# Result rows moved to partitions 30-33 and 94-97 and stored by two queues, wo's first set in two pieces, five loads in halves of 64 partitions

## The chip, the cores and the metric

The kernel runs on one core of one Trainium2 chip. The metric is the device time of one execution in microseconds. Before the change it is 218.12 us, the median of three runs (217.67 to 219.65).

## What is computed

Two sequences (B = 2) each decode one token. Attention over a window of a cached history is multiplied by a gate that comes from a small gated MLP, and the input is added:

```python
xn = _layernorm(x, axis=-1)
s = _A_ref(xn, A_k_cache, A_v_cache, A_wq, A_wo)
g = _silu(_B_ref(xn, B_w_in, B_w_sp, B_b_sp, B_w_out))
return x + s * g
```

The attention `_A_ref` has 32 query heads and 8 key and value heads of 128 elements, and looks at the last W = 4096 positions of the cache:

```python
q = (x @ wq).reshape(B, Sq, Hq, Dh)          # D = 512 -> 32 x 128
...
scores = einsum("bhqd,bhkd->bhqk", q, k) * (Dh ** -0.5)
p = _softmax(scores, axis=-1)
o = einsum("bhqk,bhkd->bhqd", p, v)
return o.reshape(B, Sq, Hq * Dh) @ wo        # 4096 -> 512
```

The gate's branch `_B_ref` takes xn through w_in (512 x 1792) and a GELU, normalizes one half of the result, scales it by w_sp and b_sp, multiplies it by the other half, and takes it through w_out (896 x 512). Everything is float32. The weights wq and wo have 8.4 MB each, and the windows of k and v 33.6 MB each. They are read once; there is next to no reuse, since only two rows are multiplied with every weight.

## The kernel before

The whole program is one pass without a loop on the chip; the Python loops are unrolled, and `InOrder` (lines 27 to 39) keeps each engine's instructions in the order in which the source writes them. Its helper's line 37 therefore stands for nearly every instruction in the profile.

**Loads.** Large loads are issued on SP's queue (`sp`). Its order is win, wout, two tiles of wq, then the tiles of k and v for the eight key heads ("units"), then wo in two sets. Tiles of win, wq, k, v and wo take turns in a ring of four buffers (`slot`, line 83; RING = 4), so that a load waits until the readers of the tile four places before it are done; wout has a place of its own. Each tile covers all 128 partitions, with one contiguous run of DRAM for each partition. Small loads (xs, which is x as two rows; wb1; x4, which is x as eight rows of 128) are issued on ACT's queue.

**Units.** For each unit, DVE transposes the k tile in four parts (`turn`, the tile kt), PE multiplies them with the prepared queries (`scores`), DVE, PE and ACT make the softmax (`probabilities`), and PE multiplies the probabilities with the v tile (`values`, into acc). `evacuate` scales acc into o, `collect` gathers o over the partitions into col, and `spread` moves the heads' outputs into oT, the weights of the product with wo. SETS (line 329) says which units share an oT: units 0 to 3, 4 and 5, 6 and 7.

**Weights of 32 columns.** The products with wo, wout and the group sums use four groups of 32 output partitions each (G = 4). Only B = 2 of 32 columns of such a weight are not zero. In hT and oT these are columns 0 and 16 of each 32, so that the results stand on partitions 32g and 32g + 16. `rowm` (line 155) has a one where the partition's number modulo 32 is the column's number; multiplied with it, the four groups of a tile are added up.

**The end.** wo's rows arrive as a first set (16 blocks for units 0 to 3, one load of 4096 KB) and a second one (16 blocks for the other units, in loads of 4, 4, 4, 2, 1 and 1 blocks), lines 476 to 485. `wo_early` multiplies whole blocks of 512 columns into part, four blocks side by side; the first 24 of the 32 blocks go that way, after the last unit's `gathered` and `spread_after`. ACT copies part to parts, PE adds its groups up into so with rowm, and the last eight blocks are added to so one quarter of the columns after another (lines 516 to 523). DVE multiplies so by the gate (which is ready long before) and adds x4, and one store on SP writes the eight rows, on partitions 0, 16, 32 and so on, to the output.

Of the kernel before, what the change touches and what calls it, by code (L numbers as in the profile page):

```python
# [9 lines left out]
F32 = mybir.dt.float32  # L10
# [4 lines left out]
P = 128  # L15
HQ, DH = 32, 128
G = 4
# [25 lines left out]
def kernel(  # L43
# [13 lines left out]
    nc = tc.nc  # L57
    pe, dve, act, sp = (InOrder(tc, e) for e in (nc.tensor, nc.vector, nc.scalar, nc.sync))
    B, _, D = x.shape
    _, HKV, SK, _ = k_cache.shape  # L60
# [7 lines left out]
    FT = FH // P  # L68
    NJ = HQ * DH // P
    DC = D // G  # L70
# [7 lines left out]
    cst = ctx.enter_context(tc.tile_pool(name="cst", bufs=1))  # L78
    ring = ctx.enter_context(tc.tile_pool(name="ring", bufs=RING))
    sb = ctx.enter_context(tc.tile_pool(name="sb", bufs=2))  # L80
    ps = ctx.enter_context(tc.tile_pool(name="ps", bufs=1, space=bass.MemoryType.PSUM))

    def slot(name, *shape):
        return ring.tile([P, *shape], F32, tag="slot", name=name)

    def bank(name, *shape):
        return ps.tile([P, *shape], F32, tag="kt", name=name, bufs=3)
# [5 lines left out]
    win = slot("win", KT, F)  # L93
    sp.dma_start(win, win_v)
    wout = cst.tile([P, FT, D], F32, tag="wout", name="wout")
    sp.dma_start(wout, w_out.rearrange("(p j) d -> p j d", p=P))
    wq_v = wq.rearrange("(p k) f -> p k f", p=P)
    wqt = []
    for a in range(0, KT, 2):
        t = slot(f"wq{a}", 2, HQ * DH)  # L100
        sp.dma_start(t, wq_v[:, a : a + 2, :])
        wqt += [t[:, 0], t[:, 1]]

    wb1 = cst.tile([1, 2], F32, tag="wb1", name="wb1")
    act.dma_start(wb1[:, 0:1], bass.AP(tensor=w_sp.tensor, offset=w_sp.offset, ap=[[1, 1], [1, 1]]))
    act.dma_start(wb1[:, 1:2], bass.AP(tensor=b_sp.tensor, offset=b_sp.offset, ap=[[1, 1], [1, 1]]))
    x4 = cst.tile([P, DC], F32, tag="x4", name="x4")
    nc.gpsimd.memset(x4, 0.0)
    by_group = [[DC, G], [D, B], [1, DC]]
    act.dma_start(x4[0 : P : P // (G * B), :], bass.AP(tensor=x.tensor, offset=x.offset, ap=by_group))  # L110

    def load(name, src, u):
        t = slot(f"{name}{u}", NT, DH)
# [16 lines left out]
    for n in range(HKV):  # L130
        p = Unit()
# [17 lines left out]
    nc.gpsimd.memset(xnT, 0.0)  # L149
    ones = cst.tile([P, P], F32, tag="ones", name="ones")  # L150
    nc.gpsimd.memset(ones, 1.0)
    hT = cst.tile([P, FT, 32], F32, tag="hT", name="hT")
    nc.gpsimd.memset(hT, 0.0)

    rowm = cst.tile([P, 32], F32, tag="rowm", name="rowm")
    dve.tensor_reduce(rowm, ident.rearrange("p (g c) -> p c g", g=G), axis=AX.X, op=ALU.add)

    def rsqrt(dst, a, tag):
# [19 lines left out]
    pt = bank("xnT_ps", KT, B)  # L178
# [39 lines left out]
    for k in range(KT):  # L218
        for n in range(G):
# [3 lines left out]
                start=(k == 0), stop=(k == KT - 1),  # L223
# [14 lines left out]
    def queries(k):  # L238
        for r in range(NR):
            for g in range(G):  # L240
                c = (r * G + g) * 512
                pe.matmul(
                    pq[r][32 * g : 32 * g + 32, :], xnT[:, k, :], wqt[k][:, c : c + 512],
                    start=(k == 0), stop=(k == KT - 1),
                )
# [14 lines left out]
    z1, z2, w2 = zT[:, 0], zT[:, 1], u[:, 0]  # L260
# [16 lines left out]
    rsqrt(mean, var, "z")  # L277
    dve.tensor_mul(z2, z2, free_ap(mean, 0, per_b))
    dve.tensor_scalar(z2, z2, wb[:, 0:1], wb[:, 1:2], op0=ALU.mult, op1=ALU.add)
    dve.tensor_mul(hT[:, :, 0 : 16 * B : 16], z1, z2)  # L280
    queries(2)
    place4 = place(4, 2)
    place2 = place(2, 4)
    py = bank("ys", D)
    for j in range(FT):
        g = j % G
        pe.matmul(py[32 * g : 32 * g + 32, :], hT[:, j, :], wout[:, j, :], start=(j < G), stop=(j + G >= FT))
    ys = sb.tile([P, D], F32, tag="o", name="ys", bufs=1)
    act.activation(ys, py, AF.Copy)
    y = bank("y", DC)  # L290
    for g in range(G):
        pe.matmul(y[32 * g : 32 * g + 32, :], rowm, ys[:, g * DC : (g + 1) * DC], start=True, stop=True)
    gate = cst.tile([P, DC], F32, tag="gate", name="gate")
    dve.tensor_scalar(gate, y, -1.0, 80.0, op0=ALU.mult, op1=ALU.min)
    act.activation(gate, gate, AF.Exp)
# [7 lines left out]
    for r in range(NR):  # L303
        src = pq[r].rearrange("p (i d) -> p i d", i=REP)
# [5 lines left out]
    for r in range(NR):  # L310
        pt = bank(f"qT_ps{r}", REP, G, 32)
# [4 lines left out]
    for j in range(G):  # L316
        pe.matmul(
            pw[:, j, :], selj[:, j].rearrange("p g c -> p (g c)"), qT.rearrange("p r g b i -> p (r g b i)"),
            start=True, stop=True,
# [10 lines left out]
    sets = {}  # L330
    for i, (kv, n, nj) in enumerate(SETS):
        o1 = cst.tile([P, B, 32], F32, tag=f"o1_{i}", name=f"o1_{i}")
        oT = cst.tile([P, nj, 32], F32, tag=f"oT_{i}", name=f"oT_{i}")
        nc.gpsimd.memset(oT, 0.0)
        for a in range(n):
            sets[kv + a] = (a, n, o1)
        sets[f"oT{i}"] = (o1, oT, nj)
# [49 lines left out]
    def values(p):  # L387
        p.acc = ps.tile([P, CH, DH], F32, tag="acc", name=f"acc{p.n}")
        n = CT // CH
        for i in range(n):  # L390
            for c in range(CH):
                t = CT * c + CH * i
                pe.matmul(
                    p.acc[32 * c : 32 * c + 32].rearrange("p a d -> p (a d)"),
                    free_ap(p.pT, 32 * CH * i + c, [[CH, 32]]),
                    p.v[:, t : t + CH, :].rearrange("p t d -> p (t d)"), start=(i == 0), stop=(i == n - 1),
                )

    def evacuate(p, split=False):
        p.o = sb.tile([P, CH, DH], F32, tag="o", name=f"o{p.n}", bufs=1)  # L400
        for a in range(CH):
            if split and a % 2:
                dve.tensor_scalar_mul(p.o[:, a, :], p.acc[:, a, :], p.w[:, a : a + 1])
            else:
                act.activation(p.o[:, a, :], p.acc[:, a, :], AF.Copy, scale=p.w[:, a : a + 1])
# [3 lines left out]
    def collect(p):  # L409
        a0, n, o1 = sets[p.n]  # L410
        if a0 == 0:
            col[0] = ps.tile([P, CH, 32], F32, tag="col", name=f"col{p.n}")
        for g in range(G):
            pe.matmul(
                col[0][32 * g : 32 * g + 32], selw[:, SL - E * a0 : SL - E * a0 + 32], p.o[:, :, 32 * g : 32 * g + 32],
                start=(a0 == 0), stop=(a0 == n - 1),
            )
        if a0 == n - 1:
            both = sb.tile([P, 32], F32, tag="both", name=f"both{p.n}", bufs=1)
            dve.reduce_sum(both, col[0].rearrange("p a j -> p j a"), axis=AX.X)  # L420
            dve.tensor_mul(o1, free_ap(both, 0, [[0, B], [1, 32]]), free_ap(ofb, 0, [[1, B], [0, 32]]))

    def spread(i):
        o1, oT, nj = sets[f"oT{i}"]
        t = {8: place2, 16: place4}[nj]
        nx = 32 // nj
        pt = bank(f"oT_ps{i}", B, nj)
        for x in range(nx):
            pe.matmul(
                pt, t[:, x].rearrange("p n h g x -> p (n h g x)"), o1[:, :, nj * x : nj * x + nj],  # L430
                start=(x == 0), stop=(x == nx - 1),
            )
        dve.tensor_copy(oT[:, :, 0 : 16 * B : 16], pt.rearrange("p b j -> p j b"))

    ends = {kv + n - 1: i for i, (kv, n, nj) in enumerate(SETS)}
    def gathered(p):
        if p is not None:
            collect(p)
# [33 lines left out]
    wo_s = []  # L472
# [3 lines left out]
    blocks = []  # L476
    for first, of in ((0, (0,)), (1, (1, 2))):
        t = slot(f"wo{first}", 16, D)
        a = 0
        for i in of:  # L480
            nj = SETS[i][2]
            for j, n in (((0, 16),), ((0, 4), (4, 4)), ((0, 4), (4, 2), (6, 1), (7, 1)))[i]:
                sp.dma_start(t[:, a : a + n, :], wo_s[i][:, j : j + n, :])
                blocks.append((t[:, a : a + n, :], sets[f"oT{i}"][1], j))
                a += n
    EARLY = 24
    done = 0

    def wo_early(n):
        nonlocal done  # L490
        t, oT, j = blocks[n]
        for a in range(t.shape[1]):
            g = done % G
            pe.matmul(
                part[32 * g : 32 * g + 32, :], oT[:, j + a, :], t[:, a, :], start=(done < G), stop=(done >= EARLY - G)
            )
            done += 1

    part = ps.tile([P, 512], F32, tag="s", name="part", bufs=2)
# [4 lines left out]
    gathered(units[-2])  # L504
    values(units[-1])
    evacuate(units[-1], split=True)
    gathered(units[-1])
    spread_after(units[-1])
    for n in range(3):
        wo_early(n)  # L510
    parts = sb.tile([P, D], F32, tag="o", name="parts", bufs=1)
    act.activation(parts, part, AF.Copy)
    so = bank("so", DC)
    for g in range(G):
        pe.matmul(so[32 * g : 32 * g + 32, :], rowm, parts[:, g * DC : (g + 1) * DC], start=True, stop=False)
    for n in range(3, len(blocks)):
        t, oT, j = blocks[n]
        for a in range(t.shape[1]):
            for g in range(G):
                pe.matmul(  # L520
                    so[32 * g : 32 * g + 32, :], oT[:, j + a, :], t[:, a, g * DC : (g + 1) * DC],
                    start=False, stop=(j + a == oT.shape[1] - 1),
                )
    res = cst.tile([P, DC], F32, tag="res", name="res")
    dve.tensor_mul(res, so, gate)
    dve.tensor_add(res, res, x4)
    sp.dma_start(bass.AP(tensor=out.tensor, offset=out.offset, ap=by_group), res[0 : P : P // (G * B), :])


# [26 lines left out]
```

## Time and profile before

| | |
|---|---|
| median of three runs | 218.12 us (217.67 to 219.65) |
| the profiled execution | 218.11 us |
| its span, first to last instruction | 216.2 us |
| mean granted TensorE clock | 0.783 |
| read from HBM | 89.40 MB |
| share of 16 DMA engines that SP's queue (q1) takes | 96.8% |
| DVE busy, PE busy | 103.9 us, 136.8 us |

The page gives, for each engine, its busy time and the share of the span. The span is then cut into 40 slices, with one digit for the busy share of each. The chain that ended last is followed back from the last instruction, each step to what released it. In the list of DMA issues the last number is the time from the issue to the landing, which includes the time that the load stood in the queue behind others. In a timeline, what stands in square brackets is the idle time of the engine before that row and what ended it.

### The profile page before, as it was taken

Reading aid. Unit: us, or ns where it says so; the run is one execution under the profiler, and the core shown is the slowest. Engines: PE = TensorE matmul, PEld = TensorE weight load, DVE = VectorE, ACT = ScalarE, POOL = GpSimd, SP = SyncE. Lnnn points to the kernel's source line nnn. Section 1 sums busy time; section 2 is a strip of 40 time slices with the busy share of each in tenths; the row PEclk is TensorE's granted clock in tenths of the full one; section 3 lists DMA queues with packets and bytes.
Section 4 is the critical chain, followed back from the end, with each engine's and each line's share of the span. In section 5 each row is a group of like instructions: output and inputs, shape, how many; then the busy total and the mean of one; then the engine's idle time right before and its main releaser. Section 6 shows DMA issues by size and latency. Waiting matters only on the chain.

```text
span 216.2 us, 2192 instructions
## 1 busy us (share of the span) xinstructions
PE 136.8 (63%) x908; PEld 46.8 (22%) x908; DVE 103.9 (48%) x161; ACT 23.9 (11%) x60; POOL 3.2 (1%) x16
## 2 busy tenths in 40 slices
PE   0172294627765964984593298359667749969683
PEld 0120021113112222222131122122221122342331
DVE  2504014439539638728908921990487197220201
ACT  5003003200001011021021002101010012030010
POOL 5000000000000000000000000000000000000000
PEclk9998569985587595596599559956955787997998
DMA  7999999999999999999999999999999999999990
GB/s 255 425 437 467 406 455 418 423 443 412 455 400 461 409 455 412 436 430 424 449 403 455 412 449 415 430 436 418 455 408 449 418 443 415 443 430 402 409 376 27
DMA packets 3929, 89.54 MB, mean 414 GB/s; under 512 B 446, under 2 KB 462, under 8 KB 848
## 3 DMA queue, kind: packets, MB, share of 16 engines
q1 hardware_dynamic: 3900, 89.40, 96.8%
q8 instruction: 7, 0.11, 0.2%
q10 hardware_dynamic: 20, 0.01, 0.0%
q14 instruction: 2, 0.02, 0.0%
HBM read 89.40 MB, written 0.00 MB: 413 GB/s over the span
## 4 chain that ended last, share of the span: by engine, by line
DMA 62%; DVE 17%; PE 17%; SPq 2%; issue 1%; ACT 0%; DVEq 0%; ACTq 0%
DMA v<-in_A_v_cache_dram 29%; DMA k<-in_A_k_cache_dram 20%; DVE kt L37 13%; DMA wo<-in_A_wo_dram 12%; PE acc L37 9%; PE s L37 7%; SPq L37 2%; PE pp L37 1%; DVE sm L37 1%; DVE pT L37 1%; DVE qw L37 1%; ACT p L37 0%; DVE mg L37 0%; DVE res L37 0%; PE so L37 0%
## 5 line engine op out<-in xcount | busy, mean ns | idle before, releaser
L37 DVE STREAM_TRANSPOSE kt<-k 128x2048 f32<-128x2048 f32 x32 | 72.7, 2293 | 3.4 <-DMA k<-in_A_k_cache_dram 3.4
L37 PE MATMUL acc<-v,pT 128*32 128x512 f32 x256 | 45.3, 863 | 10.9 <-DMA v<-in_A_v_cache_dram 9.6
L37 PE MATMUL s<-kt,qw 128*32 128x512 f32 x256 | 41.1, 684 | 3.7 <-DVE kt L37 3.1
L37 PE MATMUL pp<-p,swap 128*128 128x512 f32 x16 | 12.6, 880 | 21.0 <-ACT p L37 21.0
L37 DVE CUSTOM_DVE_ANT_1 sm<-s,own 128x512 f32<-128x512 f32 x8 | 5.5, 690 | 36.9 <-PE s L37 36.9
L37 PEld LDWEIGHTS acc<-v,pT 128*32 128x32 f32 x256 | 11.5, 159 | 37.4 <-issue 33.4
L37 ACT ACTIVATE o<-acc,wd 128x128 f32<-128x128 f32 x30 | 8.7, 368 | 73.9 <-PE acc L37 67.1
L37 PE MATMUL q_ps<-wq,xnT 128*32 128x512 f32 x64 | 9.6, 723 | 11.2 <-DMA wq<-in_A_wq_dram 11.2
L37 PEld LDWEIGHTS s<-kt,qw 128*32 128x32 f32 x256 | 9.4, 122 | 33.0 <-issue 21.9
L37 ACT ACTIVATE p<-sm,nb 128x512 f32<-128x512 f32 x8 | 5.8, 723 | 69.1 <-DVE nb L37 69.1
L37 DVE STREAM_TRANSPOSE pT<-pp 128x512 f32<-128x512 f32 x8 | 5.7, 706 | 5.8 <-PE pp L37 5.8
L37 PE MATMUL z<-win,xnT 128*32 128x448 f32 x32 | 5.6, 868 | 4.4 <-DMA win<-in_B_w_in_dram 4.4
L37 PE MATMUL mo<-mg,same 128*128 128x16 f32 x16 | 3.2, 273 | 7.7 <-DVE mg L37 7.7
L37 PEld LDWEIGHTS pp<-p,swap 128*128 128x128 f32 x16 | 3.0, 234 | 21.8 <-ACT p L37 21.8
L37 DVE TENSOR_REDUCE both<-col 128x32 f32<-128x128 f32 x3 | 0.9, 292 | 13.4 <-PE col L37 13.4
L37 PEld LDWEIGHTS mo<-l,same 128*128 128x128 f32 x16 | 4.4, 276 | 6.0 <-issue 6.0
L37 ACT ACT_TABLE_LOAD x4 | 5.1, 1283 | 2.6 <-POOL place L206 2.6
L37 PE MATMUL part<-wo,oT 128*32 128x512 f32 x48 | 5.4, 594 | 0.0
L37 PEld LDWEIGHTS q_ps<-wq,xnT 128*32 128x32 f32 x64 | 1.9, 125 | 14.7 <-DMA wq<-in_A_wq_dram 11.4
L37 PE MATMUL xnT_ps<-ident,xn 2*128 2x2 f32 x4 | 0.6, 253 | 7.0 <-DVE xn L37 7.0
L37 PE MATMUL qj_ps<-qT,selj 128*128 128x64 f32 x8 | 2.0, 428 | 4.8 <-DVE qT L37 4.8
L37 DVE STREAM_TRANSPOSE zt<-z 128x448 f32<-128x448 f32 x1 | 1.0, 975 | 8.3 <-ACT z L37 8.3
(106 smaller groups left out, 66.9 us busy)
## 6 DMA issues: line engine op xcount, KB each, us to landing
k<-in_A_k_cache_dram SPq DMA_DIRECT2D x8, 4096.0 KB, 26.4
v<-in_A_v_cache_dram SPq DMA_DIRECT2D x8, 4096.0 KB, 29.7
wq<-in_A_wq_dram SPq DMA_DIRECT2D x2, 4096.0 KB, 24.2
wo<-in_A_wo_dram SPq DMA_DIRECT2D x1, 4096.0 KB
win<-in_B_w_in_dram SPq DMA_DIRECT2D x1, 3584.0 KB, 11.1
wo<-in_A_wo_dram SPq DMA_DIRECT2D x3, 1024.0 KB, 21.7
wout<-in_B_w_out_dram SPq DMA_DIRECT2D x1, 1792.0 KB, 14.9
wo<-in_A_wo_dram SPq DMA_DIRECT2D x1, 512.0 KB
```

The lines of the kernel that those rows point to most:

```text
L37: return self.tc.keep_in_program_order(call(*args, **kwargs))
```

## The change

- The helper `halves` issues a load as two, for partitions 0 to 63 and 64 to 127. It is used for wout, both tiles of wq, and the two pieces of wo's first set, which was one load of 16 blocks and is now two of eight.
- hT, oT and rowm get 30 columns of zeros ahead of them (PAD). `turn_of` takes a window of 32 columns from them, which starts either at the padding or behind it, so that the two result rows stand on the last two partitions of an even group or on the first two of an odd one. The rows of the result are then on partitions 30 to 33 and 94 to 97.
- x4 is loaded by two issues of four rows each on ACT, and the result is stored by two of four rows, one on ACT and one on SP.
- The blocks list has one more entry, since wo's first set is two pieces. The first piece's `wo_early` moves ahead of the last unit's `gathered`; the others stay behind its `spread_after`.

```diff
--- before.py
+++ after.py
@@ -80,6 +80,10 @@
     sb = ctx.enter_context(tc.tile_pool(name="sb", bufs=2))
     ps = ctx.enter_context(tc.tile_pool(name="ps", bufs=1, space=bass.MemoryType.PSUM))
 
+    def halves(dst, src):
+        for r in (slice(0, P // 2), slice(P // 2, P)):
+            sp.dma_start(dst[r], src[r])
+
     def slot(name, *shape):
         return ring.tile([P, *shape], F32, tag="slot", name=name)
 
@@ -93,21 +97,29 @@
     win = slot("win", KT, F)
     sp.dma_start(win, win_v)
     wout = cst.tile([P, FT, D], F32, tag="wout", name="wout")
-    sp.dma_start(wout, w_out.rearrange("(p j) d -> p j d", p=P))
+    halves(wout, w_out.rearrange("(p j) d -> p j d", p=P))
     wq_v = wq.rearrange("(p k) f -> p k f", p=P)
     wqt = []
     for a in range(0, KT, 2):
         t = slot(f"wq{a}", 2, HQ * DH)
-        sp.dma_start(t, wq_v[:, a : a + 2, :])
+        halves(t, wq_v[:, a : a + 2, :])
         wqt += [t[:, 0], t[:, 1]]
 
     wb1 = cst.tile([1, 2], F32, tag="wb1", name="wb1")
     act.dma_start(wb1[:, 0:1], bass.AP(tensor=w_sp.tensor, offset=w_sp.offset, ap=[[1, 1], [1, 1]]))
     act.dma_start(wb1[:, 1:2], bass.AP(tensor=b_sp.tensor, offset=b_sp.offset, ap=[[1, 1], [1, 1]]))
+    PAD = 32 - B
+    PAIRS = ((act, 0), (sp, 2))
+    pair = lambda t, g: t[32 * g + PAD : 32 * g + PAD + 2 * B, :]
+    of_pair = lambda t, g: bass.AP(tensor=t.tensor, offset=t.offset + g * DC, ap=[[DC, 2], [D, B], [1, DC]])
     x4 = cst.tile([P, DC], F32, tag="x4", name="x4")
     nc.gpsimd.memset(x4, 0.0)
-    by_group = [[DC, G], [D, B], [1, DC]]
-    act.dma_start(x4[0 : P : P // (G * B), :], bass.AP(tensor=x.tensor, offset=x.offset, ap=by_group))
+    for _, g in PAIRS:
+        act.dma_start(pair(x4, g), of_pair(x, g))
+
+    def turn_of(t, j, g):
+        return t[:, 32 * j + PAD * (g % 2) : 32 * j + PAD * (g % 2) + 32]
+
 
     def load(name, src, u):
         t = slot(f"{name}{u}", NT, DH)
@@ -149,10 +161,12 @@
     nc.gpsimd.memset(xnT, 0.0)
     ones = cst.tile([P, P], F32, tag="ones", name="ones")
     nc.gpsimd.memset(ones, 1.0)
-    hT = cst.tile([P, FT, 32], F32, tag="hT", name="hT")
+    hT = cst.tile([P, PAD + 32 * FT], F32, tag="hT", name="hT")
     nc.gpsimd.memset(hT, 0.0)
 
-    rowm = cst.tile([P, 32], F32, tag="rowm", name="rowm")
+    rowp = cst.tile([P, PAD + 32], F32, tag="rowp", name="rowp")
+    nc.gpsimd.memset(rowp, 0.0)
+    rowm = rowp[:, PAD:]
     dve.tensor_reduce(rowm, ident.rearrange("p (g c) -> p c g", g=G), axis=AX.X, op=ALU.add)
 
     def rsqrt(dst, a, tag):
@@ -277,19 +291,19 @@
     rsqrt(mean, var, "z")
     dve.tensor_mul(z2, z2, free_ap(mean, 0, per_b))
     dve.tensor_scalar(z2, z2, wb[:, 0:1], wb[:, 1:2], op0=ALU.mult, op1=ALU.add)
-    dve.tensor_mul(hT[:, :, 0 : 16 * B : 16], z1, z2)
+    dve.tensor_mul(hT[:, PAD:].rearrange("p (j c) -> p j c", c=32)[:, :, :B], z1, z2)
     queries(2)
     place4 = place(4, 2)
     place2 = place(2, 4)
     py = bank("ys", D)
     for j in range(FT):
         g = j % G
-        pe.matmul(py[32 * g : 32 * g + 32, :], hT[:, j, :], wout[:, j, :], start=(j < G), stop=(j + G >= FT))
+        pe.matmul(py[32 * g : 32 * g + 32, :], turn_of(hT, j, 1), wout[:, j, :], start=(j < G), stop=(j + G >= FT))
     ys = sb.tile([P, D], F32, tag="o", name="ys", bufs=1)
     act.activation(ys, py, AF.Copy)
     y = bank("y", DC)
     for g in range(G):
-        pe.matmul(y[32 * g : 32 * g + 32, :], rowm, ys[:, g * DC : (g + 1) * DC], start=True, stop=True)
+        pe.matmul(y[32 * g : 32 * g + 32, :], turn_of(rowp, 0, g), ys[:, g * DC : (g + 1) * DC], start=True, stop=True)
     gate = cst.tile([P, DC], F32, tag="gate", name="gate")
     dve.tensor_scalar(gate, y, -1.0, 80.0, op0=ALU.mult, op1=ALU.min)
     act.activation(gate, gate, AF.Exp)
@@ -330,7 +344,7 @@
     sets = {}
     for i, (kv, n, nj) in enumerate(SETS):
         o1 = cst.tile([P, B, 32], F32, tag=f"o1_{i}", name=f"o1_{i}")
-        oT = cst.tile([P, nj, 32], F32, tag=f"oT_{i}", name=f"oT_{i}")
+        oT = cst.tile([P, PAD + 32 * nj], F32, tag=f"oT_{i}", name=f"oT_{i}")
         nc.gpsimd.memset(oT, 0.0)
         for a in range(n):
             sets[kv + a] = (a, n, o1)
@@ -430,7 +444,7 @@
                 pt, t[:, x].rearrange("p n h g x -> p (n h g x)"), o1[:, :, nj * x : nj * x + nj],
                 start=(x == 0), stop=(x == nx - 1),
             )
-        dve.tensor_copy(oT[:, :, 0 : 16 * B : 16], pt.rearrange("p b j -> p j b"))
+        dve.tensor_copy(oT[:, PAD:].rearrange("p (j c) -> p j c", c=32)[:, :, :B], pt.rearrange("p b j -> p j b"))
 
     ends = {kv + n - 1: i for i, (kv, n, nj) in enumerate(SETS)}
     def gathered(p):
@@ -479,8 +493,8 @@
         a = 0
         for i in of:
             nj = SETS[i][2]
-            for j, n in (((0, 16),), ((0, 4), (4, 4)), ((0, 4), (4, 2), (6, 1), (7, 1)))[i]:
-                sp.dma_start(t[:, a : a + n, :], wo_s[i][:, j : j + n, :])
+            for j, n in (((0, 8), (8, 8)), ((0, 4), (4, 4)), ((0, 4), (4, 2), (6, 1), (7, 1)))[i]:
+                (sp.dma_start if i else halves)(t[:, a : a + n, :], wo_s[i][:, j : j + n, :])
                 blocks.append((t[:, a : a + n, :], sets[f"oT{i}"][1], j))
                 a += n
     EARLY = 24
@@ -492,7 +506,7 @@
         for a in range(t.shape[1]):
             g = done % G
             pe.matmul(
-                part[32 * g : 32 * g + 32, :], oT[:, j + a, :], t[:, a, :], start=(done < G), stop=(done >= EARLY - G)
+                part[32 * g : 32 * g + 32, :], turn_of(oT, j + a, 1), t[:, a, :], start=(done < G), stop=(done >= EARLY - G)
             )
             done += 1
 
@@ -504,27 +518,29 @@
     gathered(units[-2])
     values(units[-1])
     evacuate(units[-1], split=True)
+    wo_early(0)
     gathered(units[-1])
     spread_after(units[-1])
-    for n in range(3):
+    for n in range(1, 4):
         wo_early(n)
     parts = sb.tile([P, D], F32, tag="o", name="parts", bufs=1)
     act.activation(parts, part, AF.Copy)
     so = bank("so", DC)
     for g in range(G):
-        pe.matmul(so[32 * g : 32 * g + 32, :], rowm, parts[:, g * DC : (g + 1) * DC], start=True, stop=False)
-    for n in range(3, len(blocks)):
+        pe.matmul(so[32 * g : 32 * g + 32, :], turn_of(rowp, 0, g), parts[:, g * DC : (g + 1) * DC], start=True, stop=False)
+    for n in range(4, len(blocks)):
         t, oT, j = blocks[n]
         for a in range(t.shape[1]):
             for g in range(G):
                 pe.matmul(
-                    so[32 * g : 32 * g + 32, :], oT[:, j + a, :], t[:, a, g * DC : (g + 1) * DC],
-                    start=False, stop=(j + a == oT.shape[1] - 1),
+                    so[32 * g : 32 * g + 32, :], turn_of(oT, j + a, g), t[:, a, g * DC : (g + 1) * DC],
+                    start=False, stop=(n == len(blocks) - 1 and a == t.shape[1] - 1),
                 )
     res = cst.tile([P, DC], F32, tag="res", name="res")
     dve.tensor_mul(res, so, gate)
     dve.tensor_add(res, res, x4)
-    sp.dma_start(bass.AP(tensor=out.tensor, offset=out.offset, ap=by_group), res[0 : P : P // (G * B), :])
+    for engine, g in PAIRS:
+        engine.dma_start(of_pair(out, g), pair(res, g))
 
 
 # ---- launch: one core; inputs and outputs as the reference has them ----
```

## The prediction

> **What bounds the kernel now.** I read the page first: busy shares, slices, bytes.
>
> ```profile
> span 216.2 us, 2192 instructions
> ...
> PE 136.8 (63%) x908; PEld 46.8 (22%) x908; DVE 103.9 (48%) x161; ACT 23.9 (11%) x60; POOL 3.2 (1%) x16
> ...
> DMA  7999999999999999999999999999999999999990
> ...
> HBM read 89.40 MB, written 0.00 MB: 413 GB/s over the span
> ...
> DMA 62%; DVE 17%; PE 17%; SPq 2%; issue 1%; ACT 0%; DVEq 0%; ACTq 0%
> ```
>
> No compute engine is near its limit. The DMA engines stand at nine tenths or more in 38 of 40 slices, and 62% of the chain that ended last is transfer. Where the chain passes through DVE or PE it only names what released a buffer; the engines of the DMA had other loads to move meanwhile. The table of stages makes that firm (columns: length, busy time and count of PE, PEld, DVE, ACT, POOL, granted clock, DMA share, GB/s):
>
> ```profile
> 11.00:14.00 3.00, 2.04 (x12) 0.68 (x16) 0.00 (x0) 0.00 (x0) 0.00 (x0) 1.00 0.99 425
> ...
> 24.00:34.00 10.00, 6.53 (x36) 1.83 (x36) 1.03 (x6) 1.14 (x2) 0.00 (x0) 0.68 0.99 429
> ...
> 50.00:80.00 30.00, 22.48 (x116) 6.16 (x115) 18.72 (x22) 1.95 (x6) 0.00 (x0) 0.70 1.01 433
> 80.00:110.00 30.00, 20.19 (x112) 7.01 (x116) 20.70 (x19) 2.77 (x8) 0.00 (x0) 0.66 1.00 428
> 110.00:140.00 30.00, 17.37 (x130) 6.28 (x123) 16.38 (x19) 3.91 (x12) 0.00 (x0) 0.82 1.00 431
> ...
> 200.00:212.00 12.00, 9.07 (x126) 4.10 (x128) 1.40 (x5) 1.07 (x3) 0.00 (x0) 1.00 0.90 365
> ```
>
> From 11 us on the rate is 425 to 433 GB/s with a share of about 1, whatever is being loaded. Time that a load adds or saves is therefore time of the kernel: 89.4 MB at 431 GB/s are 207.4 of the 216.2 us. The rest is the start, some idle DMA near 200 to 212 us (a tenth of 12 us, 1.2 us), and the tail. The chain in order of time shows the tail:
>
> ```profile
> 46.65 2.31 DVE kt L37
> ...
> 185.47 26.99 DMA wo<-in_A_wo_dram
> 212.46 0.04 issue
> 212.50 0.47 PE so L37 x8
> ...
> 213.00 0.30 DVE res L37
> ...
> 213.32 0.29 DVE res L37
> ```
>
> The first row is the first transpose of a k tile, which starts when that tile has landed. The last piece of wo lands at 212.46; eight matmuls and two DVE operations follow, then the store.
>
> **The five loads in halves.** Sizes, from the page's list of DMA issues (KB of 1024 bytes, then us to landing):
>
> ```profile
> wq<-in_A_wq_dram SPq DMA_DIRECT2D x2, 4096.0 KB, 24.2
> wo<-in_A_wo_dram SPq DMA_DIRECT2D x1, 4096.0 KB
> win<-in_B_w_in_dram SPq DMA_DIRECT2D x1, 3584.0 KB, 11.1
> wo<-in_A_wo_dram SPq DMA_DIRECT2D x3, 1024.0 KB, 21.7
> wout<-in_B_w_out_dram SPq DMA_DIRECT2D x1, 1792.0 KB, 14.9
> ```
>
> At 431 GB/s a load of 4096 KB (4.194 MB) takes 9.73 us and wout (1.835 MB) 4.26 us. The halved ones are wout, two of wq and wo's first set, which is now two pieces in two halves each: 4.26 + 3 x 9.73 = 33.4 us of the stream, 23.7 of it before k, 9.7 near the end.
>
> No row shows a load that reaches 64 partitions: all the large ones reach 128. So its price must be bounded. The ceiling of 431 GB/s is held either by the sixteen engines that move the bytes or by the partitions that take them, 431/128 = 3.4 GB/s for each. If the engines hold it, halves cost nothing. If the receiving side holds it, a half-load runs at half the rate; the two halves stand behind each other in one queue, whose engines must finish their share of the first before the second, and each load takes twice its time: +33.4 us. A gain at this place has no mechanism, since the share is already 0.99 in these stages and the bytes stay. I take the upper end: 3.4 GB/s is the most that any row here shows a partition to take over a long stretch, and the lower end asks for 6.7, for which there is no row. I keep both ends for the range.
>
> [...]
>
> Rows of wo's first set become 16 KB instead of 32 KB in one run. The nearest rows: wout's 14 KB rows went by in the stage 11 to 14 us and after without a dip (425), and wo's short rows in 200 to 212 gave 365/0.90 = 406 while busy, 6% less. So 0 to 0.6 us; I take 0.1, nearer to wout, whose rows are almost as long.
>
> **More issues and waits on SP.** Six more loads at some 0.5 us of SP each are 3 us in a queue that idles far longer:
>
> ```profile
> SPq L37 <- DVE kt L37: 104.1, 8, 16.1
> ...
> SPq L551 <- DMA out_dram<-res: 0.7, 1, 0.7
> ```
>
> The eight completion semaphores go round faster, so in the built program wq's second half waits for win (0.73 + 11.1 = 11.8 us), with the rest of wq and k behind it on SP; by then wout and wq's first half, 4.26 + 4.87 = 9.1 us of transfer, are still queued. Wo's last two single rows wait for the first piece's two halves, which land at least 8 us before the engines come to those rows. Both cost nothing; without that cover they would cost the whole gap.
>
> **The rows at 30-33 and 94-97.** Every matmul keeps its shape, only the columns of its 32-wide weights move. POOL gets one memset (rowp) ahead of DVE's first reduction, and ACT one more issue ahead of the first activation:
>
> ```profile
> 1.33 0.24 ACTq L37 DMA_DIRECT2D wb<-in_B_w_sp_dram  x1
> ...
> 1.60 0.27 ACTq L37 DMA_DIRECT2D wb<-in_B_b_sp_dram  x1
> ...
> 1.73 0.28 POOL L153 MEMSET hT<- 128x224 f32 x1
> 1.91 0.62 ACTq L37 DMA_DIRECT2D x<-in_A_x_dram  x1
> ...
> 11.96 5.55 PE L37 MATMUL z<-win,xnT 128*32 128x448 f32 x32 [4.35 <-DMA win<-in_B_w_in_dram]
> ```
>
> Behind them wait the layer norm's chain and xnT on DVE, ACT and PE. PE stood idle 4.35 us for win after that chain, which hides 0.28 + 0.62; without this cover they would add up to 0.9.
>
> The store: one issue of 0.69 us on SP for eight lines of 512 bytes becomes one of four lines on SP and one on ACT, side by side.
>
> ```profile
> 213.64 0.69 SPq L37 DMA_DIRECT2D out_dram<-res  x1
> ```
>
> Issues of one line took 0.24 and 0.27, of eight 0.62 and 0.69: four should take about 0.45, so -0.2 us. Bounds: -0.45 (as one line) and +0.5 (the closing wait for a landing, 0.7 in the row above, met twice in part).
>
> **wo's first piece ahead of the last gathering.** PE now does eight blocks of wo's first set before it gathers the last unit, and waits for the first piece there; behind it on PE stand col, the spread of the last set, and the remaining blocks; DVE's both and oT wait for these.
>
> ```profile
> 194.38 5.24 PE L37 MATMUL acc<-v,pT 128*32 128x512 f32 x32
> ...
> 200.92 0.35 DVE L37 TENSOR_SCALAR o<-acc,wd 128x128 f32<-128x128 f32 x1 [0.43 <-ACT o L37]
> ...
> 201.33 0.43 PE L37 MATMUL col<-o,selw 128*32 128x128 f32 x8 [1.71 <-DVE o L37]
> ...
> 203.42 5.36 PE L37 MATMUL part<-wo,oT 128*32 128x512 f32 x48
> ```
>
> Its 16 instructions take 16 x 5.36/48 = 1.8 us and fill the gap in which PE waited for o (199.62 to 201.33). At full rate the piece is there in time: the first 1024 KB piece of wo's second set lands at 183.1 + 21.7 = 204.9 or so (it is issued one SP step after 182.7), the whole first set 2.4 us earlier, its first half 4.9 us before that, at 197.6. At half rate everything up to v's last load is 23.7 us later, acc ends at 223.3, the piece lands at 197.6 + 23.7 + 4.9 = 226.2, and PE waits 2.9 us; col to the start of part is 2.1 us, so all but the second piece is done near 230, that piece lands at 235.9, and the last row of wo at 212.46 + 33.4 = 245.9. The transfer hides this wait by many us, so it costs nothing, and the 1.8 us brought forward gain nothing either: the end still hangs on wo's last row and eight matmuls.
>
> **The sum.** 216.2 + 33.4 + 0.1 - 0.2 = 249.5 us of span. The profiled execution took 218.11 us, 1.9 more than its span and the same as the median 218.12, so **251.4 us**.
>
> **Rivals.** First, on the other side: the engines hold the ceiling, not the partitions, or the halves are dealt to different engines and move together. Then nothing is added: 216.2 + 0.1 - 0.2 + 1.9 = 218.0, with -0.45 to +1.1 for the store and the shorter rows: 217.5 to 219.2. For it: the share and rate are the same for every length of row and every source, as a limit of the engines would be. Against it: the same rows fit a limit of the receiving side just as well, and no row has a partition above 3.4 GB/s. It decides from the first halved load, wout.
>
> Second: two engines that write to the same partitions are served one after the other, not in turn. One then runs ahead by a half-load, the pair works on opposite halves from there on, and the loss is paid once: 4.9 us in wq, up to 2.4 more in wo's shorter halves; 218.0 + 4.9 to 218.0 + 7.3, at most 225.3. For it: the loads of one queue need no common step, as the steady share shows. Against it: nothing shows who would be preferred.
>
> Third: a gain beyond the store. The idle 1.2 us in 200 to 212 and the 0.45 of the store together give 1.65, 216.5; there is no more to win, so over 1% faster (2.2 us) hardly can be.
>
> **Numbers.** A measurement of this kernel tells about 1% from no change: its three runs reach from 217.67 to 219.65. Forecast 0.56, the engines' limit 0.33, loss paid once 0.08, a gain 0.03. I put the forecast ahead because it extends the rate that the rows show for a partition, and not far ahead, because the same rows permit the other. The forecast's own range is 246.0 to 252.5 (engines that are already out of step lose somewhat less; 0.6 for the rows and 0.5 for the store above). Its chance alone doesn't hold 8 in 10, so the range must reach over to the first rival: 217.2 to 252.5. Slower by over 1%: 0.56 + 0.08 = 0.64; within 1%: 0.33; faster: 0.03.
>
> **What would show it.** Right: slices 3 to 8 of the page near 215 GB/s with the DMA share still at nine tenths, wq landing some 24 us later, k's first transpose near 70 us instead of 46.65, and a second dip after v's last load. Wrong: 425 GB/s through these slices, z and q at the same times as before, and an end near 216 us; a store issue not below 0.6 us would make its step wrong alone.

## The result, and the profile after

The changed kernel takes 255.14 us (median of six runs, 253.53 to 256.11) against 218.2 us before: a ratio of 1.168, 95% interval 1.162 to 1.173. The forecast had the direction and the place; the time lies 2.6 us above its range. Ratios and intervals here and below leave out executions over 1.5% above the fastest of their kernel. The profiled execution took 255.21 us, its span is 253.4 us.

The page of the changed kernel, with busy shares, slices, bytes and the chain's shares:

```profile
span 253.4 us, 2208 instructions
...
PE 138.8 (55%) x908; PEld 48.0 (19%) x908; DVE 103.9 (41%) x161; ACT 23.9 (9%) x60; POOL 3.3 (1%) x17
...
DMA  7999999898999999999999999999999999999991
GB/s 290 363 225 240 212 202 222 191 228 275 460 432 419 419 434 442 434 424 419 440 445 422 424 429 437 445 424 419 429 441 440 416 419 429 202 215 219 256 404 45
...
HBM read 89.40 MB, written 0.00 MB: 353 GB/s over the span
...
DMA 65%; PE 16%; DVE 14%; issue 1%; ACT 1%; SPq 1%; another core or an unknown queue 0%; DVEq 0%
```

The bytes are the same, DVE's busy time is the same to a tenth, and the DMA engines look as busy as before. What fell is what they move: some 190 to 240 GB/s in slices 3 to 9, where wout and wq are loaded, and 202 to 256 in slices 35 to 38, where wo's first set is. A row of nines for the DMA engines does not say that they move all they can; it has to be read beside the row of GB/s.

The stages (length, busy time and count of PE, PEld, DVE, ACT, POOL, granted clock, DMA share, GB/s) say the same more sharply:

```profile
24.00:34.00 10.00, 0.00 (x0) 0.00 (x0) 0.00 (x0) 0.00 (x0) 0.00 (x0) 0.50 1.02 213
34.00:44.00 10.00, 2.93 (x16) 0.68 (x16) 0.00 (x0) 0.00 (x0) 0.00 (x0) 0.52 1.00 210
...
104.00:134.00 30.00, 17.31 (x104) 6.30 (x107) 20.37 (x19) 2.77 (x8) 0.00 (x0) 0.69 0.99 428
...
224.00:234.00 10.00, 5.95 (x40) 1.52 (x32) 0.89 (x3) 0.73 (x2) 0.00 (x0) 0.67 0.99 211
```

From 24 to 34 us not one instruction ran on a compute engine, with the DMA share at 1.02 and half the rate of the kernel before (429 in the same stage). Between the two places, in 104 to 134 us, the whole loads run at 428 as ever. The chain in order of time shows where k's first tile is used, and the end:

```profile
14.60 46.61 DMA wq<-in_A_wq_dram
...
70.69 2.31 DVE kt L37
...
229.56 19.78 DMA wo<-in_A_wo_dram
249.34 0.04 issue
249.38 0.47 PE so L37 x8
...
250.20 0.29 DVE res L37
```

k's first transpose starts at 70.69 instead of 46.65, 24.0 later; wo's last row lands at 249.34 instead of 212.46, 36.9 later. The chain passes from wo to wo at 229.56 because SP waited there for a completion semaphore that one of the first pieces still held, and issued wo's last row only then. That wait is no cost: with the share at 0.99 the engines had other rows to move. The tail has its own row in the timeline:

```profile
250.52 0.78 SPq L37 DMA_DIRECT2D out_dram<-res  x1
250.52 0.66 ACTq L37 DMA_DIRECT2D out_dram<-res  x1
```

From the store's issue to the end of the span are 253.4 - 250.5 = 2.9 us, against 216.2 - 213.6 = 2.6 before.

### The profile page after: what moved, and what is told of

Same layout as the page of the kernel before. It is cut to its first block, busy times and chain, and to the rows that moved or that the text cites. A ratio compares the mean times of both kernels' runs of the same rounds, so it can differ in the third digit from the quotient of the medians.

```text
span 253.4 us, 2208 instructions
## 1 busy us (share of the span) xinstructions
PE 138.8 (55%) x908; PEld 48.0 (19%) x908; DVE 103.9 (41%) x161; ACT 23.9 (9%) x60; POOL 3.3 (1%) x17
## 4 chain that ended last, share of the span: by engine, by line
DMA 65%; PE 16%; DVE 14%; issue 1%; ACT 1%; SPq 1%; another core or an unknown queue 0%; DVEq 0%
DMA v<-in_A_v_cache_dram 25%; DMA wq<-in_A_wq_dram 18%; DMA wo<-in_A_wo_dram 17%; DVE kt L37 10%; PE acc L37 7%; PE s L37 5%; DMA win<-in_B_w_in_dram 5%; PE pp L37 1%; PE q_ps L37 1%; DVE pT L37 1%; DVE sm L37 1%; DVE gate L37 1%; PE ys L37 1%; ACT p L37 1%; SPq L37 1%
## 5 line engine op out<-in xcount | busy, mean ns | idle before, releaser
L37 PE MATMUL acc<-v,pT 128*32 128x512 f32 x256 | 44.6, 860 | 15.0 <-DMA v<-in_A_v_cache_dram 14.4
L37 PE MATMUL s<-kt,qw 128*32 128x512 f32 x256 | 38.8, 653 | 4.5 <-DVE kt L37 3.1
L37 PE MATMUL q_ps<-wq,xnT 128*32 128x512 f32 x64 | 10.4, 780 | 37.2 <-DMA wq<-in_A_wq_dram 37.2
L37 PEld LDWEIGHTS acc<-v,pT 128*32 128x32 f32 x256 | 11.4, 158 | 41.8 <-issue 36.6
L37 PE MATMUL part<-wo,oT 128*32 128x512 f32 x48 | 9.9, 987 | 7.4 <-DMA wo<-in_A_wo_dram 7.4
L37 PE MATMUL z<-win,xnT 128*32 128x448 f32 x32 | 4.6, 731 | 5.2 <-DMA win<-in_B_w_in_dram 5.2
L37 DVE TENSOR_TENSOR res<-so,gate 128x128 f32<-128x128 f32 x1 | 0.3, 290 | 13.3 <-PE so L37 13.3
```

The lines of the kernel that those rows point to most:

```text
L37: return self.tc.keep_in_program_order(call(*args, **kwargs))
```

## The experiments

Each kernel was timed beside the kernel before on the same chip. Edits are against the changed kernel where nothing else is said.

### All but the halves

```diff
     def halves(dst, src):
-        for r in (slice(0, P // 2), slice(P // 2, P)):
-            sp.dma_start(dst[r], src[r])
+        sp.dma_start(dst, src)
```

> All of the change but the halves: wout, both tiles of wq and the two pieces of wo's first set are each one load again. Receiving side (a load to partitions 0-63 or 64-127 runs at half rate, and this is the whole cost): 218.2 + 0.3 for the tail, which is 0.3 us longer in the profile of the changed kernel, so 218.5, between 217.8 and 219.3, and 425 to 435 GB/s in every slice. Rival (the 3.7 us beyond the forecast come from the rest: the wait for wo's first piece ahead of the last gathering, the faster round of the semaphores, the moved rows): 221 to 222.

Measured: 218.47 us against 218.15, ratio 1.001 (0.9994 to 1.0026). The stage of wq is back at its rate:

```profile
24.00:34.00 10.00, 6.82 (x36) 1.91 (x36) 1.03 (x6) 0.96 (x2) 0.00 (x0) 0.66 0.99 429
```

So the halves are the whole loss, and the 3.7 us beyond the forecast are theirs too. The moved rows, the two stores, the two pieces and the earlier matmuls together cannot be told from nothing.

### The early halves alone, and the late ones alone

```diff
-                (sp.dma_start if i else halves)(t[:, a : a + n, :], wo_s[i][:, j : j + n, :])
+                sp.dma_start(t[:, a : a + n, :], wo_s[i][:, j : j + n, :])
```

> Halves only in wout and wq; wo's two pieces are whole. Receiving side: k's later tiles stood 25.1 us later in the changed kernel than before, so 218.5 + 25.1 = 243.6 (242.5 to 244.5), and the DMA share stays near 1 while the rate is about 210 GB/s. By the forecast's sizes alone: 218.5 + 23.7 = 242.2.

Measured: 243.48 us, ratio 1.115 (1.111 to 1.119); 25.0 us more than without any halves.

```diff
-    halves(wout, w_out.rearrange("(p j) d -> p j d", p=P))
+    sp.dma_start(wout, w_out.rearrange("(p j) d -> p j d", p=P))
...
-        halves(t, wq_v[:, a : a + 2, :])
+        sp.dma_start(t, wq_v[:, a : a + 2, :])
```

> Halves only in the two pieces of wo's first set. By the forecast's size: 218.5 + 9.7 = 228.2. If the late part of the changed kernel is as large by itself (36.9 - 25.0 = 11.9 us between v's sixth load and the last of wo): 230.4, with v's last load landing about 2 us later than the load before it lets expect.

Measured: 229.86 us (227.33 to 230.66), ratio 1.051 (1.044 to 1.057); 11.4 us more than without halves. The two add up: 25.0 + 11.4 = 36.4 of the 36.7 us between the changed kernel and the one without halves. Each is more than the forecast's size, by 1.3 and 1.7 us. For the late halves the time lies between the two that were expected. The stages in which v's last load ends and wo's halves begin, of the kernel with the late halves:

```profile
186.00:190.00 4.00, 2.45 (x16) 0.72 (x8) 0.33 (x2) 1.79 (x6) 0.00 (x0) 1.00 0.97 406
190.00:194.00 4.00, 3.86 (x20) 2.73 (x20) 1.18 (x4) 0.05 (x1) 0.00 (x0) 0.61 1.02 209
194.00:198.00 4.00, 3.72 (x20) 1.11 (x24) 0.00 (x0) 0.00 (x0) 0.00 (x0) 0.53 1.04 225
```

Already from 190 to 194 us, while the last rows of v's last load, a whole one, still come in, the rate is down to half.

### Sixty-four rows elsewhere

Is a load of 64 rows slow by itself, or by where its rows land?

```diff
     def halves(dst, src):
-        for r in (slice(0, P // 2), slice(P // 2, P)):
+        for r in (slice(32, 96), slice(0, 32), slice(96, P)):
             sp.dma_start(dst[r], src[r])
```

> The five loads in three instead of two: partitions 32-95, then 0-31, then 96-127. The first is again 64 rows, but half of them stand in 0-63 and half in 64-127. Receiving side by halves of the partitions: 32-95 goes at full rate (half of a load's time), each quarter at half rate (half of a load's time each): 1.5 times the time, + 16.7 us, 235.2, up to 239 with losses at the borders. Rival (a load of 64 rows is slow wherever it lands, for the DRAM side or for four rows per engine): 32-95 takes the whole time of a load and the quarters at least half each: 2 times or more, 255 or above.

Measured: 240.74 us, ratio 1.102 (1.098 to 1.106): 22.3 us more than whole loads, less than the 36.7 of the halves, more than the 16.7 that half rate for the quarters alone would make, and 1.7 above the highest time that was expected for it. Two stages of this kernel, the first with the 64 rows in the middle on their way, the second with quarters:

```profile
18.50:21.50 3.00, 0.00 (x0) 0.00 (x0) 1.76 (x10) 1.51 (x2) 0.00 (x0) 0.59 1.09 470
25.00:29.00 4.00, 0.00 (x0) 0.00 (x0) 0.00 (x0) 0.00 (x0) 0.00 (x0) 0.50 0.81 180
```

The rates of such short stages are rough, since a row of 32 KB counts where it starts, but one is full and the other is half or less. A finer measure is the single row: the trace records each row (a load's bytes for one partition) that one of the sixteen engines moves, with its length and its time, and adding these times up and dividing by 16 gives what a load takes of the stream. For each tile of wq the load of the middle took 5.5 us of the stream, where 64 rows of a whole load take 4.85, and the two quarters took 4.9 us each instead of 2.4. In the middle most rows took 1.21 to 1.22 us, as in a whole load; it was an engine's first row behind a quarter that took longer (1.8 us, median). So partitions 32 to 95 can be filled at full rate by a load of 64 rows, and a part of that is lost again at the borders: the middle loads of wo's two pieces took 3.1 and 4.2 us instead of 2.45. That is where the time beyond the expected one lies.

```diff
-        for r in (slice(0, P // 2), slice(P // 2, P)):
+        for r in (slice(0, P, 2), slice(1, P, 2)):
```

> The five loads in halves again, but of every other partition (0, 2, 4 ... and 1, 3, 5 ...): 64 rows that are spread over all partitions. Receiving side: both groups of 64 are reached by each load, so most of the loss goes; engines that take consecutive rows can still meet at the same partitions' entrance for a part of the time, so 218.5 to 236. Rival (64 rows per load are slow by themselves): about 255.

Measured: 218.18 us against 218.1, ratio 0.9998 (0.998 to 1.001). The rates in the page of this kernel, and two of its stages:

```profile
GB/s 255 425 437 467 406 443 430 426 440 400 461 406 461 409 455 412 437 437 418 455 397 461 406 455 415 443 424 437 437 414 449 409 443 424 437 397 426 420 374 21
```

```profile
24.00:34.00 10.00, 6.07 (x36) 1.69 (x36) 1.03 (x6) 1.44 (x2) 0.00 (x0) 0.73 1.01 436
...
190.00:200.00 10.00, 8.79 (x68) 3.67 (x68) 1.53 (x5) 1.83 (x6) 0.00 (x0) 0.83 0.98 414
```

The same number of loads, with 64 rows of the same length each, at the same places in the queue, cost nothing when they take every other partition. That excludes the number of rows, the number of loads, the rows that an engine gets, and the semaphores. It leaves where in the 128 partitions the rows land. The source rows moved along with the partitions in both variants, so a limit on the DRAM's side that follows the same pattern is not excluded by these two alone; it wasn't tried apart. What speaks against it is that rows of 8, 14, 16 and 32 KB, from three tensors, all took close to twice their time in halves (on average a row of 8 KB 0.6 us instead of 0.31, one of 14 KB 1.05 instead of 0.54, one of 16 KB 1.24 instead of 0.62, one of 32 KB 2.5 instead of 1.21).

### Both halves at once, from two queues

```diff
     def halves(dst, src):
-        for r in (slice(0, P // 2), slice(P // 2, P)):
-            sp.dma_start(dst[r], src[r])
+        for engine, r in ((sp, slice(0, P // 2)), (act, slice(P // 2, P))):
+            engine.dma_start(dst[r], src[r])
```

wo's pieces are whole here.

> As e2 (halves in wout and wq, wo's pieces whole: 243.5), but the halves for partitions 64-127 are issued on ACT's queue, so that both halves of a load stand ahead of each engine at once. Receiving side, engines in step with each other (all take a row of the one half, then a row of the other): no gain, 242 to 245. Receiving side, engines that fall out of step of themselves, so that some write low partitions while others write high ones: down to 218.5 at best, and somewhere between with partial overlap. Rival (64 rows are slow by themselves): 243.5 or more.

Measured: 241.91 to 245.87 us in four executions, of which the lower two (241.91 and 244.77) give the ratio 1.115 (1.109 to 1.121), the same as with both halves on SP (1.115). Two stages of the profiled execution, which took 245.87 us:

```profile
30.00:40.00 10.00, 0.61 (x4) 0.55 (x4) 1.15 (x6) 2.97 (x4) 0.00 (x0) 1.00 1.07 242
40.00:50.00 10.00, 4.53 (x32) 1.15 (x32) 3.05 (x12) 0.54 (x1) 0.00 (x0) 0.99 0.97 216
```

ACT's first activation came only at 34.9 us, behind its loads, so that the layer norm's chain ran from there on; but the DMA share stayed near 1, and the transfers set the time. With both halves at hand the engines did not spread over low and high partitions, or only a little: while halves of both queues were under way, from 35 to 48 us, a row of 32 KB took 2.26 us (median), against 2.57 once SP's halves were alone and 1.21 in a whole load. What that gained was lost elsewhere: win, a whole load on SP, now ran beside ACT's halves, and took 13.3 us of the stream instead of 9.2.

### Finer pieces, and borders

```diff
-            for j, n in (((0, 8), (8, 8)), ((0, 4), (4, 4)), ((0, 4), (4, 2), (6, 1), (7, 1)))[i]:
+            for j, n in (((0, 4), (4, 4), (8, 4), (12, 4)), ((0, 4), (4, 4)), ((0, 4), (4, 2), (6, 1), (7, 1)))[i]:
```

wout and wq are whole, and the calls of `wo_early` count two pieces more.

> As e3 (halves in wo's first set only: 229.9), but the set in four pieces of four blocks instead of two of eight, each in halves: the same bytes to each half, eight half-loads of 512 KB instead of four of 1024. If the loss is half rate for the bytes plus one border after v's last load: as e3, 229 to 231. If every change from low to high partitions costs something: 231 to 233. If engines that are 2 us apart are already at the next half while others finish the last (a half of 512 KB lasts 1.2 us at full rate): less than e3, 222 to 227.

Measured: 229.25 us (226.81 to 230.96, the highest of four not in the ratio), ratio 1.047 (1.042 to 1.051), not to be told from 1.051 (1.044 to 1.057). So the loss goes by the bytes and not by the number of halves; changing from low to high partitions inside a run of halves costs nothing that shows. What is left is the change from whole loads to halves. With the same four pieces, two of them whole:

```diff
-                (sp.dma_start if i else halves)(t[:, a : a + n, :], wo_s[i][:, j : j + n, :])
+                (halves if i == 0 and j in (0, 4) else sp.dma_start)(t[:, a : a + n, :], wo_s[i][:, j : j + n, :])
```

> wo's first set in four pieces of four blocks; the first two in halves, the last two whole (2.1 MB in halves, entered once from whole loads, right behind v's last). What is open is where the 1.7 us come from that e3 lost beyond half rate (11.4 for 9.7). Rate alone: 218.5 + 4.9 = 223.4. In proportion to the bytes (11.4/9.7): 224.2. A loss of 1.7 at the entry, where engines that are ahead meet engines that still write v: 225.1.

and with `(0, 8)` in the place of `(0, 4)`:

> The same four pieces, and the first and the third in halves, the second and the fourth whole: the same bytes in halves as e9, entered twice. Rate alone or in proportion to the bytes: the same time as e9. A loss at each entry: 1.7 us more than e9, 226.8.

Measured: 224.69 us, ratio 1.032 (1.030 to 1.033), with one run of halves, and 227.71 us, ratio 1.045 (1.042 to 1.048), with two. The same bytes, the same number of loads, only their order differs, and it is worth 3.0 us between the medians (1.5 between the two profiled executions, 224.34 and 225.84). One run alone does not tell a loss in proportion to the bytes (224.2) from a loss at the border (225.1); the second run does. The stages of the first of the two, then of the second:

```profile
190.00:194.00 4.00, 3.40 (x24) 2.28 (x27) 1.17 (x4) 0.00 (x0) 0.00 (x0) 0.66 0.98 223
194.00:198.00 4.00, 4.00 (x24) 1.05 (x20) 0.00 (x0) 0.00 (x0) 0.00 (x0) 0.50 1.02 234
198.00:202.00 4.00, 2.74 (x32) 0.67 (x24) 1.01 (x4) 0.74 (x2) 0.00 (x0) 0.99 1.02 221
202.00:206.00 4.00, 2.88 (x20) 1.33 (x24) 0.39 (x2) 0.00 (x0) 0.00 (x0) 0.87 0.98 401
```

```profile
190.00:194.00 4.00, 2.37 (x20) 1.59 (x20) 1.17 (x4) 0.00 (x0) 0.00 (x0) 0.86 0.96 207
194.00:198.00 4.00, 3.46 (x20) 0.98 (x24) 0.00 (x0) 0.00 (x0) 0.00 (x0) 0.50 1.01 215
198.00:202.00 4.00, 3.60 (x28) 0.86 (x20) 0.35 (x1) 0.72 (x2) 0.00 (x0) 0.78 1.02 256
202.00:206.00 4.00, 2.49 (x24) 1.28 (x24) 1.04 (x4) 0.01 (x1) 0.00 (x0) 1.00 1.03 225
206.00:210.00 4.00, 1.98 (x12) 0.28 (x15) 0.00 (x0) 0.00 (x0) 0.00 (x0) 0.57 0.97 365
```

The first is back at 401 from 202 us on. In the second the piece between the two halved ones is whole, 1.05 MB, 2.4 us at full rate, and no stage shows it: 256 is the best. The single rows do show it. A row of 8 KB took 0.31 us undisturbed. In the first kernel it took 0.57 and 0.58 us on average in the two halved pieces, 0.45 in the whole piece behind them and 0.31 in the next one. In the second it took 0.61 in the first halved piece, 0.52 in the whole one between, 0.60 in the second halved one and 0.45 in the whole one behind. (The record of a row does not name its engine; the pieces are told apart by following rows from the end of one to the start of the next.)

So whole loads that stand next to halves lose too. The sixteen engines are not at the same place in the queue: in the second kernel the first halved row of wo starts at 189.8 us, and the last row of v, a whole load, ends at 193.4 us. Of the rows of v still under way in between, the slowest took 2.3 to 2.5 us instead of 1.21. That whole rows are slowed while halved ones are under way is measured; which rows meet at which partitions no record shows, so this last step stays an inference.

### The store alone

Against the kernel before, with the rows where they were:

```diff
-    sp.dma_start(bass.AP(tensor=out.tensor, offset=out.offset, ap=by_group), res[0 : P : P // (G * B), :])
+    for engine, g in ((act, 0), (sp, 2)):
+        engine.dma_start(
+            bass.AP(tensor=out.tensor, offset=out.offset + g * DC, ap=[[DC, 2], [D, B], [1, DC]]),
+            res[32 * g : 32 * g + 64 : P // (G * B), :],
+        )
```

> The kernel before, with its store alone in two: four lines on ACT's queue and four on SP's, from the partitions where they were. By the forecast the issue of four lines takes about 0.45 us instead of 0.69: 0.2 us faster, 218.0. By the profile of the changed kernel, where the two issues took 0.78 and 0.66: no gain, 218.2 to 218.5, and the issues take 0.65 to 0.8 again.

Measured: 218.44 us against 218.1, ratio 1.0015 (0.9997 to 1.0033): no gain. Its timeline:

```profile
213.62 0.67 SPq L37 DMA_DIRECT2D out_dram<-res  x1
213.62 0.61 ACTq L37 DMA_DIRECT2D out_dram<-res  x1
```

Issues of four lines take 0.61 and 0.67 us, as one of eight did (0.69).

## Why the prediction was wrong

**The bound was read rightly.** Everything that the transfers lost came out at the end: 25.0 us of the early part were not made up in the 150 us of work behind it, and the compute engines' longer waits cost nothing. The rate, given as 425 to 433 GB/s from 11 us on, was in fact 460 from 14 to 24 us and 423 from 34 to 50 us; the bound does not hang on that.

**The halves: half rate was right, its reason wrong, the size too small.** The step that failed is the term "each load takes twice its time: +33.4 us". In its place stand 36.4 us: 25.0 for wout and wq where 23.7 stood, 11.4 for wo where 9.7 stood. The rows' times, in us of the stream, say where they are, in the kernel without halves and in the changed one:

| rows | without halves | changed | more |
|---|---|---|---|
| wout, in halves | 4.28 | 8.36 | 4.1 |
| wq, in halves | 19.41 | 39.95 | 20.5 |
| wo's first set, in halves | 9.86 | 19.83 | 10.0 |
| k and v, whole | 155.96 | 157.15 | 1.2 |
| wo's second set, its rows of 8 KB, whole | 7.53 | 8.96 | 1.4 |

The sum is 37.2, half a microsecond more than the 36.7 by the measured times. The halved loads take 34.6 of it instead of 33.4, mainly because wq takes 2.06 times its time: 210 to 213 GB/s instead of 431/2 = 215.5. The whole loads beside them take 2.6, which the prediction put at nothing. Each part alone shows the same: with the early halves only, wout and wq take 24.9 us more and the loads beside them 0.5; with the late ones only, wo's first set takes 9.6 us more, as forecast, and the loads beside it 1.9. So the early 1.3 us beyond the forecast are wq's own rows, and the late 1.7 are the whole loads of v and wo.

A second run of halves cost 3.0 us with the same bytes, and one run with 2.1 MB of halves lost 224.69 - 218.47 - 4.9 = 1.3 us beyond half rate. In the range I had even let engines that are out of step lose less, and set its upper end by the rows' length and the store alone; the runs show the opposite sign, and 252.5 was too low for these two reasons.

**The ends of the bound.** The choice between them was right, the reason for it was not. The lower end, where the sixteen engines alone set the rate of any load, fell with the rate of 213 at a share of 1.02. But the upper end was chosen because no row showed a partition above 3.4 GB/s, and that is no limit: with every other partition, 64 of them were filled at 436 GB/s, an estimated 436/64 = 6.8 GB/s each, and partitions 32 to 95 went at full rate too (most rows of 32 KB took 1.21 to 1.22 us there, as in a whole load). By the prediction's working those loads would have cost the same 33.4 us as the halves, and loads of every other partition cost nothing. What fits the runs in its place, an estimate from them that no row shows by itself, is a limit of some 213 GB/s for the low 64 partitions and as much for the high 64, each as a group, and not one of each partition: halves went at 210 to 213, and a quarter of a tile of wq, 1.05 MB in 4.9 us, at 214 as well. That the change cuts its loads just there is luck in this step, and the number came near because of it.

**wo's rows of 16 KB** were forecast at 0.1 us; the kernel with the two pieces whole stands at 1.001 (0.9994 to 1.0026), which has room for it and for up to 0.6 us.

**SP's issues and the semaphores** cost nothing, as forecast: the kernel with as many loads, each of every other partition, stands at 0.9998. In the changed kernel SP's waits for the reused semaphores show in the chain at 229.56 and nowhere in the rate (211 GB/s in 224 to 234 us; wq's stages had 210 to 213).

**The layer norm's chain** behind the added memset and issue stayed hidden, as the kernel without halves shows (1.001).

**The store** was forecast 0.2 us faster and is not: the time of an issue hardly goes down with its lines from eight to four (0.69 to 0.61 and 0.67). The error was a straight line drawn from one line (0.24 to 0.27) to eight (0.62 to 0.69).

**wo's first piece ahead of the gathering.** I forecast that PE would wait 2.9 us for the piece and that the second piece would cover it. The timeline of the changed kernel:

```profile
219.94 5.93 PE L37 MATMUL acc<-v,pT 128*32 128x512 f32 x32 [2.64 <-DMA v<-in_A_v_cache_dram]
...
229.68 3.64 PE L37 MATMUL part<-wo,oT 128*32 128x512 f32 x16 [3.81 <-DMA wo<-in_A_wo_dram]
...
239.85 6.21 PE L37 MATMUL part<-wo,oT 128*32 128x512 f32 x32 [3.55 <-DMA wo<-in_A_wo_dram]
```

PE waited 3.81 us, and 3.55 us again for the second piece at 239.85: what was held up in between was done before it could matter. The forecast was right here: the wait is 0.9 us longer than forecast and cost nothing.

**The rivals.** No cost at all fell with the result. The loss paid once (225.3 at most) fell too, and with it the idea behind it: neither with one queue nor with two, both halves at hand, did the engines part of their own accord by more than a small part (a row of 32 KB took 2.26 us with halves of both queues under way, 2.57 with those of one, and 1.21 in a whole load). A gain from the store fell with the kernel that has only that.

## What to carry to other kernels

In a kernel that lives from its transfers, look at which partitions a load covers before looking at its size: here 64 rows on neighbouring partitions from 0 or from 64 went at half rate (210 to 213 GB/s), 64 rows on every other partition at full rate (436 GB/s), and most rows on 32 to 95 in a whole load's 1.21 to 1.22 us. Read the share of the DMA engines only beside the GB/s, since it stood at 1.02 when the rate was 213. A slow stretch in a stream was dearer than its bytes say, because the loads next to it lost as well (a row of 8 KB in the whole piece behind took 0.45 us instead of 0.31), so that one run of such loads was cheaper than two (224.69 us against 227.71).

## What the runs showed of the hardware that I had not expected

Loads of 64 rows on every other partition, two to a tile, ran at 436 GB/s and cost nothing (0.9998, 0.998 to 1.001). Loads of 64 neighbouring partitions from 0 or from 64 ran at 210 to 213. For every other partition I had expected 218.5 to 236 us; it was 218.18.

The order of the same loads was worth 3.0 us (1.032 against 1.045). And an issue of a store of four lines took as long as one of eight, 0.61 to 0.78 us against 0.69.
